# Ten input loads issued as 121 rows and 7 rows instead of 128 rows at once

## Chip, cores and metric

The kernel runs on one core of one Trainium2 chip. Its time is the device time of that core in microseconds (us); lower is better. Five engines work side by side on one program, each in its own order: PE (matmul, with its weight loads PEld), DVE, ACT, POOL, and SP, which in this kernel only issues DMAs. The core has 16 DMA engines that move the data.

## What is computed

For 8 batches, 12 heads, 448 positions and a head size of 64, all in float32 at the borders:

```python
scores = scale * np.matmul(q, k.transpose(0, 1, 3, 2)) - np.log(S)
attn = 1.0 / (1.0 + np.exp(-scores))
x = np.matmul(attn, v)            # heads side by side: x is [8, 448, 768]
wq = x @ w_q                      # [8, 448, 64]
wk = x @ w_k
W_tok = scale * np.einsum('bsd,btd->bst', wq, wk)
mixed = np.einsum('bst,btd->bsd', W_tok, x)
out = np.maximum(mixed, 0.0) @ w_out
```

## The kernel before

The 12 heads of a batch are taken four at a time, which gives 24 quads, n = 0 to 23. For each quad the kernel loads q, k and v (448 KB each, float32), casts them to bfloat16 (mostly on POOL), brings q and k into transposed form (transposes on PE or DVE), and makes seven blocks of scores: PE multiplies (line 328), one ACT instruction per block takes the sigmoid of 128 x 896 numbers out of PSUM (line 333), and PE multiplies the result with v (line 350). When three quads of a batch are done, the token-mixing part of that batch follows, and its output is stored.

The order of the work on every engine is written out by hand. The string `PLAN` gives one letter per step, `ORDER` gives the order of the loads and of their casts, and `BANKS` names the PSUM banks. "k5" below is the k load of quad 5.

Loads go through `load1`, which `pump_loads` calls on SP. A load is one DMA of 128 rows, 3.5 KB to a row: line 177 for q and k of the quads that are transposed on DVE (each row one piece of 896 numbers), line 188 for v and the other q and k (each row two pieces of 448 numbers). All loads share a pool of 8 buffers (`p_ld`), so a load is issued only when the load eight places before it has been cast:

```python
            if len(ring) >= 8 and ring[-8] not in cast:
                break
```

SP works in order: a DMA that has to wait holds up all DMAs behind it, including the loads, the copies of the output weights (`wout<-wout`, line 878) and the stores of the output.

The framework adds one more rule, which the source doesn't show. Each DMA that SP or ACT issues signals its landing on one of eight semaphores, called DMAHW0 to DMAHW7 in the lists below, and these are handed out in rotation, one per DMA. A DMA waits until the DMA that had its semaphore before it has landed. So no more than eight of these DMAs are under way at a time.

The cast of a load waits for all DMAs that fill its buffer. POOL casts at line 201 (q and k of the quads transposed on DVE), line 224 (other q and k) and line 218 (v). The weights `w_out` come in by two DMAs that POOL issues (line 670), on a queue of their own.

Of the kernel before, what the change touches and what calls it, by code (L numbers as in the profile page):

```python
# [17 lines left out]
def kernel(  # L18
# [17 lines left out]
    P = 128  # L36
    NI, NP = 7, 64
# [112 lines left out]
    SRC = dict(q=q, k=k, v=v)  # L150
# [3 lines left out]
    def arrange(n, eng):  # L154
# [12 lines left out]
        for g in range(2):  # L167
            lo = slice(64 * g, 64 * g + 32)
            eng.tensor_copy(out=w[lo, 1], in_=z[lo])  # L169

    def load1(n, nm, eng):
        u, j = quads[n]
        if KIND[n] in "cer" and nm != "v":
            t = p_ld.tile([P, 2 * RUN + PAD], F32, tag="ld", name=nm + "32")
            t = t[:, 0 : 2 * RUN] if n < SPLIT else t.rearrange("p (y x) -> p y x", y=2)[:, :, 0:RUN]
            rows = SRC[nm][u, 4 * j : 4 * j + 4]
            eng.dma_start(
                out=t,
                in_=rows.rearrange("h (p r) d -> (h p) (r d)", r=2 * NI)
                if n < SPLIT else rows.rearrange("h (p y r) d -> (h p) y (r d)", y=2, r=NI),  # L180
            )
            ld[nm, n] = (
                t.rearrange("p (y i e d) -> p e y i d", y=2, i=NI, e=2)
                if n < SPLIT else t.rearrange("p y (i e d) -> p e y i d", i=NI, e=2)
            )
            return
        t = p_ld.tile([P, 2, NI * HD], F32, tag="ld", name=nm + "32")
        eng.dma_start(
            out=t,
            in_=SRC[nm][u, 4 * j : 4 * j + 4].rearrange(  # L190
                "(g h) (p i) d -> (h p) g (i d)", g=2, i=NI
            ),
        )
        ld[nm, n] = t

# [486 lines left out]
    def cols(r):  # L682
# [9 lines left out]
        out=ident, in_=ident, compare_op=ALU.not_equal, fill=1.0, base=0,  # L692
# [35 lines left out]
    def pump_loads():  # L728
        while len(loaded) < len(ORDER):

            late = len(ring) > LATE
            if late and not allowed[0]:
                break
            nm, n = ORDER[len(loaded)]
            if nm == "w" and n or (nm, n) in CASTING:
                loaded.add((nm, n))
                continue
            if len(ring) >= 8 and ring[-8] not in cast:
                break
            allowed[0] -= late  # L740
            ring.append((nm, n))
            if nm == "w":
                load_weights()
            else:
                load1(n, nm, nc.sync)
            loaded.add((nm, n))
# [81 lines left out]
    for t in PLAN:  # L828
# [17 lines left out]
        elif kind == "P":  # L846
            n, i = divmod(c, NI)
# [17 lines left out]
        elif t == "z":  # L865
            n = quads_r.pop(0)
# [16 lines left out]
        elif kind == "M":  # L883
            u, x = divmod(c, NC // 2)
# [48 lines left out]
```

## Time and profile before

| | |
|---|---|
| median of 3 runs | 182.57 us (180.17 to 185.29) |
| profiled execution, span from first to last instruction | 180.1 us |
| busy in the span | PE 169.6, ACT 159.0, DVE 145.6, POOL 121.4 us |
| moved by DMA | 47.31 MB, mean 263 GB/s |
| granted TensorE clock | full throughout |

The profile gives no time of the profiled execution beside its span; the span lies at the lowest of the three timed runs. The profile's time line lists instructions in order of time as: start, duration, engine, line, what is written and read, count, and in brackets the idle time just before it and what ended that idle time. The view of stretches gives busy times of each engine between two points in time. The DMA view gives, for each group of issues, the count, the size and the median time from issue to landing.

### The profile page before, as it was taken

The page shows a single profiled execution, that of the slowest core. Times are in us where ns is not written, and L with a number is a line of the kernel's source. Part 1 is how long each engine was busy: PE and PEld are TensorE (multiplying, and loading weights), DVE is VectorE, ACT ScalarE, POOL GpSimd, SP SyncE. Part 2 cuts the span into 40 slices and gives each one's busy share as a digit, 9 for nine tenths or more (in the row PEclk, how much of TensorE's full clock was granted, in tenths as well). Part 3 has the DMA queues.
Part 4 walks back from the last instruction along what each step waited for, and adds up shares of the span by engine and source line. Part 5 has one row for each costly group of instructions (what it writes and reads, how often), then busy time and mean ns, then how long its engine had stood idle before and what let it go on. Part 6 is the DMA issues. An engine that isn't in the chain of part 4 may idle for free.

```text
span 180.1 us, 7907 instructions
## 1 busy us (share of the span) xinstructions
PE 169.6 (94%) x3440; PEld 112.2 (62%) x3440; DVE 145.6 (81%) x227; ACT 159.0 (88%) x208; POOL 121.4 (67%) x166
## 2 busy tenths in 40 slices
PE   7698899889899999999999999999999999999990
PEld 3334445444575555445667786678887788888660
DVE  3578899997989896889999999979898886768351
ACT  4699999999899999999999999999999989976300
POOL 1028799689999999999999999979979910010000
PEclk9999999999999999999999999999999999999999
DMA  5999999999999998899998889987795523505876
GB/s 177 355 372 349 322 383 381 280 302 356 342 294 349 339 265 267 217 319 365 343 300 315 217 288 305 342 322 213 200 338 173 135 64 73 137 4 122 201 208 175
DMA packets 27475, 47.31 MB, mean 263 GB/s; under 512 B 3888, under 2 KB 23600, under 8 KB 27440
## 3 DMA queue, kind: packets, MB, share of 16 engines
q1 hardware_dynamic: 26160, 44.64, 78.0%
q0 software_dynamic: 800, 1.18, 3.6%
q10 hardware_dynamic: 480, 0.98, 1.5%
q8 instruction: 27, 0.44, 1.0%
q14 instruction: 8, 0.07, 0.1%
HBM read 35.78 MB, written 11.01 MB: 260 GB/s over the span
## 4 chain that ended last, share of the span: by engine, by line
PE 56%; POOL 16%; DMA 15%; DVE 5%; ACT 2%; issue 2%; SPq 1%; POOLq 0%
PE banks L539 15%; PE banks L350 10%; PE banks L328 10%; PE banks L620 8%; DMA q<-in_q_dram 6%; POOL qk L201 5%; DMA w<-in_moe_w_k_dram 4%; DMA k<-in_k_dram 3%; POOL qk L169 3%; DMA wout<-wout 2%; ACT at L333 2%; POOL v L218 2%; PE banks L579 2%; PE banks L413 2%; POOL swap L163 2%
## 5 line engine op out<-in xcount | busy, mean ns | idle before, releaser
L333 ACT ACTIVATE at<-banks 128x896 bf16<-128x896 f32 x168 | 140.0, 948 | 3.4 <-PE banks L328 3.0
L328 PE MATMUL banks<-qk 64*64 64x448 bf16 x672 | 62.2, 358 | 3.3 <-ACT at L333 1.6
L350 PE MATMUL banks<-at,v 64*64 64x448 bf16 x672 | 47.3, 351 | 0.8 <-ACT at L333 0.7
L328 PEld LDWEIGHTS <-qk 64*64 64x64 bf16 x672 | 25.9, 105 | 20.7 <-issue 13.2
L539 PE MATMUL banks<-wout,mx 64*64 64x384 bf16 x672 | 36.6, 323 | 0.0
L201 POOL CAST qk<-k 128x896 bf16<-128x896 f32 x19 | 22.8, 1199 | 10.6 <-DVE qk L302 9.7
L350 PEld LDWEIGHTS <-v 64*64 64x64 bf16 x672 | 23.2, 107 | 8.6 <-issue 1.7
L539 PEld LDWEIGHTS <-mx 64*64 64x64 bf16 x672 | 23.3, 107 | 4.5 <-issue 0.5
L359 DVE CAST xt<-banks 128x896 bf16<-128x896 f32 x22 | 23.8, 1083 | 2.3 <-PE banks L350 1.8
L620 PE MATMUL banks<-wout,mx 128*128 128x384 bf16 (+1 forms) x138 | 24.4, 320 | 0.0
L480 DVE TENSOR_SCALAR mx<-banks 128x1024 bf16<-128x1024 f32 (+3 forms) x22 | 21.3, 972 | 1.9 <-PE banks L493 0.7
L201 POOL CAST qk<-q 128x896 bf16<-128x896 f32 x17 | 20.4, 1198 | 2.6 <-DMA q<-in_q_dram 1.3
L218 POOL CAST v<-v 128x896 bf16<-128x896 f32 x22 | 20.6, 950 | 1.4 <-DMA v<-in_v_dram 0.4
L620 PEld LDWEIGHTS <-mx 128*128 128x128 bf16 x138 | 12.3, 98 | 9.8 <-issue 3.2
L285 DVE STREAM_TRANSPOSE qk<-qk 128x448 f32<-128x448 f32 x28 | 17.0, 627 | 0.4 <-POOL qk L166 0.3
L163 POOL COPY swap<-qk 32x448 uint32<-32x448 uint32 x28 | 15.5, 554 | 2.3 <-DVE qk L201 0.7
L166 POOL COPY qk<-qk 32x448 uint32<-32x448 uint32 x28 | 15.8, 566 | 1.6
L169 POOL COPY qk<-swap 32x448 uint32<-32x448 uint32 x28 | 15.8, 564 | 1.6
L254 DVE STREAM_TRANSPOSE qk<-qk 32x448 f32<-32x448 f32 x24 | 15.3, 636 | 0.6
L422 POOL COPY wq<-wqk 64x448 bf16<-64x448 bf16 x3 | 1.7, 555 | 15.7 <-DVE wqk L421 15.7
L653 DVE COPY o<-banks 128x384 f32<-128x384 f32 x12 | 6.6, 553 | 5.7 <-PE banks L620 5.3
L653 ACT COPY o<-banks 128x384 f32<-128x384 f32 x9 | 4.4, 490 | 7.1 <-PE banks L620 6.9
(91 smaller groups left out, 206.5 us busy)
## 6 DMA issues: line engine op xcount, KB each, us to landing
q<-in_q_dram SPq DMA_DIRECT2D x24, 448.0 KB, 6.6
v<-in_v_dram SPq DMA_DIRECT2D x24, 448.0 KB, 6.3
k<-in_k_dram SPq DMA_DIRECT2D x23, 448.0 KB, 7.0
out_dram<-o SPq DMA_DIRECT2D x50, 192.0 KB, 3.9
wout<-in_moe_w_out_dram POOLq DMA_DIRECT2D x2, 576.0 KB, 12.2
wout<-wout SPq DMA_DIRECT2D x12, 96.0 KB, 6.2
out_dram<-o ACTq DMA_DIRECT2D x4, 192.0 KB, 3.5
k<-in_k_dram SPq DMA_DIRECT2D x1, 256.0 KB, 5.6
```

The costliest lines, as they stand in the source:

```text
L163: eng.tensor_copy(out=z[lo], in_=w[hi, 0])
L169: eng.tensor_copy(out=w[lo, 1], in_=z[lo])
L201: COPY[e](out=f[:, :, "qk".index(nm)].rearrange("p e i d y -> p e y i d"), in_=ld.pop((nm, n)),)
L218: COPY[e](out=t16.rearrange("p b i d -> p (b i d)"), in_=ld.pop((nm, n)).rearrange("p b x -> p (b x)"),)
L285: nc.vector.transpose(out=qk[n][:, t].rearrange("p t i n -> p (t i n)").bitcast(F32), in_=w)
L328: nc.tensor.matmul(sc[HALF[h], g, 0:S], qk[n][HALF[g], h, 1, i, :], qk[n][HALF[g], h, 0].rearrange("p i n -> p (i n)"), start=True, stop=True,
L333: inst = nc.scalar.activation(at, sc[:, :, 0:S], ACTF.Sigmoid, bias=attn_bias, scale=attn_scale)
L350: nc.tensor.matmul(ps[HALF[g], h, 0:S], ld["v16", n][HALF[h], g, i, :], ats[n, i][HALF[h], g, :], start=(i == 0), stop=(i == NI - 1),)
L359: read(fb, COPY[eng](out=xt(u, j)[:, :, 0:S], in_=ps[:, :, 0:S]))
L480: inst = nc.vector.tensor_scalar(dst, ps, moe_scale, 0.0, ALU.mult, ALU.max)
L539: nc.tensor.matmul(ps[HALF[x], y, 0:NB], mx[HALF[y], u, b, 64 * (i - 3 * y) : 64 * (i - 3 * y) + 64], wout16[HALF[y], slot(y, b), x * NB : ...
L620: nc.tensor.matmul(ps, mxs[w][:, 2 * S * c + m * P : 2 * S * c + (m + 1) * P], wout16[:, c, w0:w1], start=(c == 0), stop=(c == NC - 1),)
```

## The change

A load named in `THIN` is issued as two DMAs, rows 0 to 120 and rows 121 to 127, into the same buffer. All other loads stay as they are. The ten are k3, k5, q6, v5, v6, k8, v8, v9, k12 and v10.

```diff
+    THIN = "k3 k5 q6 v5 v6 k8 v8 v9 k12 v10".split()
+    CUT = 121
+
+    def load_rows(nm, n, eng, dst, rows):
+
+        if f"{nm}{n}" not in THIN:
+            eng.dma_start(out=dst, in_=rows)
+            return
+        for r in (slice(0, CUT), slice(CUT, P)):
+            eng.dma_start(out=dst[r], in_=rows[r])
...
-            eng.dma_start(
-                out=t,
-                in_=rows.rearrange("h (p r) d -> (h p) (r d)", r=2 * NI)
+            load_rows(
+                nm, n, eng, t,
+                rows.rearrange("h (p r) d -> (h p) (r d)", r=2 * NI)
...
-        eng.dma_start(
-            out=t,
-            in_=SRC[nm][u, 4 * j : 4 * j + 4].rearrange(
-                "(g h) (p i) d -> (h p) g (i d)", g=2, i=NI
-            ),
-        )
+        load_rows(
+            nm, n, eng, t, SRC[nm][u, 4 * j : 4 * j + 4].rearrange("(g h) (p i) d -> (h p) g (i d)", g=2, i=NI),
+        )
```

The order of instructions on PE, DVE, ACT and POOL stays the same. SP has ten more DMAs, and from the first split load on the eight semaphores fall to other DMAs. On SP, around quad 5 to 9, the rows before are these (v5, q7, v6, q8, k8, k9, q9; the brackets name what each waits for, its own landing semaphore among it):

```order
L188 DMA v_444<-in_v_dram 128x2x448 [waits DMAHW7_49,Pool_49]
L177 DMA q_478<-in_q_dram 128x896 [waits DMAHW0_49,Pool_49]
L188 DMA v_481<-in_v_dram 128x2x448 [waits DMAHW1_49,Pool_49]
L177 DMA q_486<-in_q_dram 128x896 [waits DMAHW2_49,Pool_49]
L177 DMA k_504<-in_k_dram 128x896 [waits DMAHW3_49,Pool_49]
L177 DMA k_662<-in_k_dram 128x896 [waits DMAHW4_49,Pool_49]
L177 DMA q_666<-in_q_dram 128x896 [waits DMAHW5_49,Pool_49]
```

The same loads on SP after the change, v5, v6 and k8 in two parts each:

```order
L180 DMA v_447<-in_v_dram 121x2x448 [waits DMAHW2_49,Pool_49]
L180 DMA v_447<-in_v_dram 7x2x448 [waits DMAHW3_49]
L177 DMA q_482<-in_q_dram 128x896 [waits DMAHW4_49,Pool_49]
L180 DMA v_485<-in_v_dram 121x2x448 [waits DMAHW5_49,Pool_49]
L180 DMA v_485<-in_v_dram 7x2x448 [waits DMAHW6_49]
L177 DMA q_491<-in_q_dram 128x896 [waits DMAHW7_49,Pool_49]
L180 DMA k_509<-in_k_dram 121x896 [waits DMAHW0_49,Pool_49]
L180 DMA k_509<-in_k_dram 7x896 [waits DMAHW1_49]
L177 DMA k_668<-in_k_dram 128x896 [waits DMAHW2_49,Pool_49]
L177 DMA q_672<-in_q_dram 128x896 [waits DMAHW3_49,Pool_49]
```

The load k9 (k_662 before, k_668 after) had DMAHW4 and waited for the DMA eight places before it, the load q6. It now has DMAHW2, which the 121 rows of v5 had before it, so it waits for the landing of a load that stands only five loads ahead of it.

## The prediction

> **What bounds the kernel now.** I read the busy shares first, then the time line of the engine that is nearest to full, then the engines that feed it. The first lines of the page:
>
> ```profile
> span 180.1 us, 7907 instructions
> PE 169.6 (94%) x3440; PEld 112.2 (62%) x3440; DVE 145.6 (81%) x227; ACT 159.0 (88%) x208; POOL 121.4 (67%) x166
> DMA  5999999999999998899998889987795523505876
> ```
>
> PE and ACT are both nearly full over the whole span, so the next question is who is full when. The DMA row (40 slices of 4.5 us, tenths of the 16 engines) says that the DMA engines are full from 5 us to about 70 us, which is the part where the ten loads lie. The time line of ACT for this part:
>
> ```profile
> 9.17 39.00 ACT L333 ACTIVATE at<-banks 128x896 bf16<-128x896 f32 x48 [0.21 <-PE banks L328]
> 48.65 13.22 ACT L333 ACTIVATE at<-banks 128x896 bf16<-128x896 f32 x16 [0.48 <-PE banks L328]
> 62.22 1.73 ACT L333 ACTIVATE at<-banks 128x896 bf16<-128x896 f32 x2 [0.34 <-PE banks L328]
> ```
>
> ACT takes 48 sigmoids in 39.00 us without a gap, from 9.17 to 48.17, and then idles 0.48 us. Stretches of the span tell who takes over (the columns are the stretch, its length, the busy us of PE, PEld, DVE, ACT and POOL, clock, DMA share, GB/s):
>
> ```profile
> core 0: us, PE busy (x) PEld busy (x) DVE busy (x) ACT busy (x) POOL busy (x), PEclk, DMA share, GB/s
> 25.00:30.00 5.00, 4.85 (x74) 2.75 (x75) 4.76 (x9) 5.00 (x7) 5.00 (x6) 1.00 1.05 384
> ...
> 50.00:170.00 120.00, 119.86 (x2607) 85.33 (x2598) 102.47 (x150) 112.70 (x150) 87.76 (x121) 1.00 0.78 241
> ```
>
> From 50 to 170 us PE is busy 119.86 of 120.00 us. So **ACT sets the pace to 48 us and PE from 50 us on**. Both are full, and what comes earlier than it comes now buys almost nothing: of ACT's idle time before PE takes over there are 0.21 + 0.48 = 0.69 us, with the 0.34 at 62 us 1.03 us. That is the ceiling of any gain by faster loads in this execution.
>
> What comes later is another matter. POOL casts the loads, and its time line shows who waits for whom:
>
> ```profile
> 15.74 0.93 POOL L224 CAST k<-k 128x896 bf16<-128x896 f32 x1 [0.35 <-DMA k<-in_k_dram]
> ...
> 17.90 1.21 POOL L201 CAST qk<-k 128x896 bf16<-128x896 f32 x1 [0.18 <-DMA k<-in_k_dram]
> ...
> 20.64 0.93 POOL L218 CAST v<-v 128x896 bf16<-128x896 f32 x1 [0.40 <-DMA v<-in_v_dram]
> 22.33 2.17 POOL L769 CAST wqk<-w 64x384 bf16<-64x384 f32 x4 [0.76 <-DMA w<-in_moe_w_k_dram]
> ...
> 36.33 1.20 POOL L201 CAST qk<-q 128x896 bf16<-128x896 f32 x1 [1.29 <-DMA q<-in_q_dram]
> ...
> 44.76 1.21 POOL L201 CAST qk<-k 128x896 bf16<-128x896 f32 x1 [0.30 <-DMA k<-in_k_dram]
> ```
>
> Six times between 15 and 45 us POOL stands idle until a load lands, 3.28 us in all, and the last of these (k9, at 44.76) is the last of the first half. Until then the casts run at the pace of the DMA engines; after it no cast up to 80 us waits for a load. The short way from that last wait to ACT: DVE waits for the cast of k9 and q9, and PE and ACT come right after.
>
> ```profile
> 44.49 1.17 DVE L278 STREAM_TRANSPOSE qk<-qk 128x448 f32<-128x448 f32 x2 [1.07 <-POOL qk L201]
> ```
>
> DVE idles 1.07 us here, within 4 us of ACT's 0.48. So the time has little slack against **later** landings near 45 us: what k9 and q9 lose there, ACT loses too, and PE behind it.
>
> **The change part by part: the issue.** Ten more DMAs on SP. One issue costs about what these rows of SP show (start, duration):
>
> ```profile
> 5.64 0.38 SPq L188 DMA_DIRECT2D k<-in_k_dram  x1
> 12.18 0.37 SPq L188 DMA_DIRECT2D v<-in_v_dram  x1
> ...
> 24.53 0.37 SPq L188 DMA_DIRECT2D v<-in_v_dram  x1
> 25.80 0.34 SPq L177 DMA_DIRECT2D q<-in_q_dram  x1
> ...
> 29.52 1.20 SPq L177 DMA_DIRECT2D k<-in_k_dram  x2
> ```
>
> That is 10 x 0.38 = 3.8 us of SP, in ten places. SP waits for casts and landings most of the time (6.2 us between the two rows at 5.64 and 12.18), and a load takes far longer to land than that, because a queue of loads stands before it. I take 0. If the queue were empty, each issue would cost its 0.38 us.
>
> **The bytes per DMA engine.** A load of 448 KB is 128 rows; spread over 16 engines that is 8 rows, 28 KB, on each. At 384 GB/s (the stretch 25 to 30) one engine moves 24 GB/s, so a load costs each engine 448 x 1024 / 384 = 1.19 us and one row costs 0.15 us. How 121 and 7 rows are spread no row of the trace shows: every load in it has 128 rows. The ends: if the rows are dealt out one by one, no engine has more than 9 rows, and a split load costs at most 0.15 us more. If only equal shares are made, 121 = 11 x 11 gives 11 engines 11 rows each and the 7 rows go one each to seven engines. If these are seven of the eleven, seven engines carry 12 rows instead of 8 (+4 x 0.15 = **+0.60 us** per split load), four carry 11 (+0.45), and five carry none (-1.19). I take the second, the dearer end, since no row excludes it. [...]
>
> Six of the ten (k3, k5, q6, v5, v6, k8) go ahead of k9. The extra of k3 falls into SP's pause before 12.18, in which the engines work off the queue, so five count: 5 x 0.60 = **3.0 us** more on seven engines by the time that k9 lands. The other four (v8, v9, k12, v10) come when no cast waits for a load: 0.
>
> Against that stands work that is not a load. The page's third part:
>
> ```profile
> q1 hardware_dynamic: 26160, 44.64, 78.0%
> ...
> q8 instruction: 27, 0.44, 1.0%
> ```
>
> The 27 fetches of instructions are 16 KB each and took 1.0% of 16 x 180.1 us, so 28.8 / 27 = 1.07 us of one engine each, one every 6.7 us: seven by 45 us, about as much as a load's share each. A load has landed when its last engine is done. If the engine that has the fetches is always the same, it is up to 7 us behind the others less what it makes good in pauses, and it is this engine that ends the waits of POOL. If it is one of the five that are spared, five split loads take 5 x 1.19 = 6.0 us off it. That all loads then come earlier by 1 to 2 us until 42 us, and k9 with the +3.0 of the seven others about when it does now, is my estimate. The gain in time is small either way: between 0 and the 0.48 us of ACT at 48.65. I take half, **-0.25 us**.
>
> **The eight semaphores.** The two halves of a load use up two of them, so SP looks less far ahead. k9 now waits for v5. The DMA view for v5 (issued 24.53) and k9 (the second of the pair at 29.52, so 30.4) and the smallest load in the empty queue at the start:
>
> ```profile
> v<-in_v_dram SPq DMA_DIRECT2D x1, 448.0 KB, 9.5
> ...
> k<-in_k_dram SPq DMA_DIRECT2D x1, 448.0 KB, 14.2
> ...
> k<-in_k_dram SPq DMA_DIRECT2D x1, 192.0 KB, 3.4
> ```
>
> v5 lands at 34.0, so k9 is issued 3.6 us later than at 30.4. In this trace it landed at 44.6, behind q7, v6, q8 and k8: 4 x 1.19 = 4.8 us of queued work on the engines that carry all of it, more than the 3.4 us in which a load lands from an empty queue. I take 0; the price, if the cover were gone, is at most the 3.6 us. Behind k9 on SP wait q9, v7 and q10, then the copies of the weights, which PE doesn't read in this part.
>
> **Sum.** 0 (issue) - 0.25 (landings) + 0 (semaphores) on the profiled span of 180.1. The median of the runs is 2.47 us above that span; I put the difference onto the median: 182.57 - 0.25 = 182.3.
>
> **The rivals.**
> - *The slow side: the extra rows pace the casts.* If the engine with the fetches is one of the eleven, nothing is relieved. It carries the fetches and the extra rows, k9 and q9 land 3.0 us later, DVE, PE and ACT have no slack there: +3.0, so 185.6. With the semaphores' cover gone instead, +3.6: 186.2; with both, +6.6: 189.2. It decides from the point where k9 lands later than 44.7, when POOL already waits for it. For it speaks that five of sixteen engines are fewer than eleven; against it that an engine behind the others has less to do in each pause of SP.
> - *The relief reaches further.* The median run is 2.4 us above the fastest. If in such a run ACT waits for late loads, the relief would give part of that back: up to 182.57 - 2.4 = 180.2. Nothing in this trace shows such a run.
> - *No uneven spread.* Rows dealt out evenly: 5 x 0.15 = 0.75 us at most on some engines, nothing on the path but that: 182.6 to 183.3.
>
> **How the numbers follow.** The forecast, within 1.0 us of the median, has 0.50; even spread 0.13; the slow rival 0.25, half of it past 186.2; the far relief 0.12. Two per cent (3.65 us) is about what a measurement of this kernel can tell from no change, since its runs spread by 2.8%. That gives slower 0.14 (half of the slow rival, and a little for the spread of the runs), faster 0.07 (part of the far relief, with the spread in its favour), same 0.79. The range goes from the far relief, 180.0 with the span itself as its floor, to the slow rival with one of its prices, 186.2; beyond lie some 0.12 above and 0.05 below.
>
> **What would show it.** Right: SP with 10 more DMAs; POOL's wait before the cast of q7 (1.29 us) shorter, its wait for k9 about the same; ACT's gap near 48 us between 0 and 0.7; PE full from 50 to 170. The slow rival would show as POOL waits for loads of over 1 us at 40 to 47 and an ACT gap of 2 us or more near 48. Even spread would show as landings unchanged to 0.2 us. I am wrong if the time moves by more than 3.65 us, above all if PE is no longer full after 50 us.

## The result and the profile after

The change takes **196.63 us** (median; 193.0 to 199.75), the kernel before in the same measurement 182.63 us (180.17 to 185.29). The ratio is **1.0705, with a 95% interval of 1.0638 to 1.0773**: 7% or 12.9 us slower, and far outside the predicted 180.0 to 186.2. The ratio leaves out runs that were disturbed, and the profiled execution of the change (197.57 us) is one of them, while the undisturbed runs took 193.0 to 195.69 us.

The first part of its page (span, busy time of the engines, DMA row in 40 slices), and from the fifth part the sigmoid:

```profile
span 195.8 us, 7921 instructions
PE 174.5 (89%) x3439; PEld 117.2 (60%) x3440; DVE 145.2 (74%) x227; ACT 160.6 (82%) x208; POOL 122.2 (62%) x166
...
DMA  6999999999997689999999988997879533603875
...
L341 ACT ACTIVATE at<-banks 128x896 bf16<-128x896 f32 x168 | 141.7, 934 | 17.3 <-PE banks L336 16.7
```

(The lines are eight higher here: L333 is now L341, L328 is L336, L201 is L209, L218 is L226, L224 is L232.) The same group of before:

```profile
L333 ACT ACTIVATE at<-banks 128x896 bf16<-128x896 f32 x168 | 140.0, 948 | 3.4 <-PE banks L328 3.0
```

The engines do the same work, but ACT stands idle ahead of its sigmoids for 17.3 us instead of 3.4. These 13.9 us are most of the 15.7 us by which the span grew. Where they lie, ACT's time line of the change says (the bracket is the idle time and its releaser):

```profile
9.05 1.73 ACT L341 ACTIVATE at<-banks 128x896 bf16<-128x896 f32 x2 [0.23 <-PE banks L336]
...
20.54 14.12 ACT L341 ACTIVATE at<-banks 128x896 bf16<-128x896 f32 x17 [1.29 <-PE banks L336]
...
42.65 8.45 ACT L341 ACTIVATE at<-banks 128x896 bf16<-128x896 f32 x10 [4.10 <-PE banks L336]
52.25 4.30 ACT L341 ACTIVATE at<-banks 128x896 bf16<-128x896 f32 x5 [1.15 <-PE banks L336]
...
58.43 0.92 ACT L341 ACTIVATE at<-banks 128x896 bf16<-128x896 f32 x1 [1.88 <-PE banks L336]
```

Where before one run of 48 sigmoids went from 9.17 to 48.17 without a gap, there are now pieces. POOL, which casts the loads, shows what they wait for:

```profile
18.70 0.94 POOL L232 CAST k<-k 128x896 bf16<-128x896 f32 x1 [1.62 <-DMA k<-in_k_dram]
...
36.35 0.94 POOL L232 CAST q<-q 128x896 bf16<-128x896 f32 x1 [2.01 <-DMA v<-in_v_dram]
...
46.26 1.20 POOL L209 CAST qk<-q 128x896 bf16<-128x896 f32 x1 [1.22 <-DMA q<-in_q_dram]
...
54.44 2.31 POOL L209 CAST qk<-k 128x896 bf16<-128x896 f32 x2 [1.08 <-DMA k<-in_k_dram]
```

All four wait for landings, for 1.1 to 2.0 us (the second is the cast of q6, where the profile names the landing of a v load). The first is k3, cast at 15.74 before: 3.0 us later. The pair at 54.44 is k8, one of the ten, and k9. Before, k9 was cast at 44.76, and k8 at 43.25 without a wait:

```profile
43.25 1.20 POOL L201 CAST qk<-k 128x896 bf16<-128x896 f32 x1
```

Both come some **11 us later**, and now it is the landing of k8 that POOL waits for. The transposes on DVE at 55.67 (44.49 before) start when the cast of k8 ends, and wait 2.86 us for POOL instead of 1.07:

```profile
55.67 1.17 DVE L286 STREAM_TRANSPOSE qk<-qk 128x448 f32<-128x448 f32 x2 [2.86 <-POOL qk L209]
```

In stretches of the span (length, busy us of PE, PEld, DVE, ACT, POOL, clock, DMA share, GB/s), of the change:

```profile
25.00:45.00 20.00, 15.55 (x258) 8.32 (x253) 14.89 (x21) 15.21 (x19) 12.28 (x15) 0.85 1.02 260
40.00:45.00 5.00, 4.46 (x94) 2.95 (x94) 3.04 (x3) 2.21 (x3) 2.58 (x3) 0.50 1.04 242
62.00:182.00 120.00, 118.05 (x2594) 86.63 (x2587) 99.51 (x147) 111.63 (x148) 87.88 (x120) 0.98 0.78 236
```

and the first of them in the kernel before:

```profile
25.00:45.00 20.00, 18.54 (x358) 9.69 (x358) 18.27 (x26) 20.00 (x26) 17.59 (x22) 1.00 1.08 335
```

This pair of rows holds the answer's outline. The DMA engines are as busy as before (1.02 against 1.08), but move 260 GB/s instead of 335: a byte costs 335/260 x 1.02/1.08 = 1.22 times as much of their time. The change adds no bytes. After PE has waited, the granted clock is lower as well: 0.50 from 40 to 45 us, though PE is busy again for 4.46 of these 5.00 us. From 62 us on PE is full again (118.05 of 120.00 us), and the loss is not made good.

### The profile page after: what moved, and what is told of

Read it like the earlier page. It is cut to its first block, busy times and chain, and to the rows that moved or that the text cites. A ratio compares the mean times of both kernels' runs of the same rounds, so it can differ in the third digit from the quotient of the medians.

```text
span 195.8 us, 7921 instructions
## 1 busy us (share of the span) xinstructions
PE 174.5 (89%) x3439; PEld 117.2 (60%) x3440; DVE 145.2 (74%) x227; ACT 160.6 (82%) x208; POOL 122.2 (62%) x166
## 4 chain that ended last, share of the span: by engine, by line
PE 56%; DMA 32%; POOL 6%; SPq 2%; issue 1%; DVE 1%; POOLq 0%; DVEq 0%
PE banks L547 14%; DMA k<-in_k_dram 14%; DMA q<-in_q_dram 11%; PE banks L336 10%; PE banks L358 10%; PE banks L628 9%; DMA v<-in_v_dram 8%; PE banks L587 2%; PE banks L421 2%; PE banks L380 2%; PE banks L396 1%; PE banks L477 1%; PE banks L433 1%; PE banks L501 1%; POOL qk L209 1%
## 5 line engine op out<-in xcount | busy, mean ns | idle before, releaser
L341 ACT ACTIVATE at<-banks 128x896 bf16<-128x896 f32 x168 | 141.7, 934 | 17.3 <-PE banks L336 16.7
L336 PE MATMUL banks<-qk 64*64 64x448 bf16 x672 | 65.9, 374 | 5.1 <-DVE xn L409 2.4
L358 PE MATMUL banks<-at,v 64*64 64x448 bf16 x672 | 49.6, 363 | 2.3 <-POOL v L226 1.8
L336 PEld LDWEIGHTS <-qk 64*64 64x64 bf16 x672 | 27.3, 108 | 22.5 <-issue 14.6
L358 PEld LDWEIGHTS <-v 64*64 64x64 bf16 x672 | 25.4, 110 | 9.0 <-POOL v L226 2.9
L209 POOL CAST qk<-k 128x896 bf16<-128x896 f32 x19 | 22.7, 1200 | 12.6 <-DMA k<-in_k_dram 11.2
L628 PE MATMUL banks<-wout,mx 128*128 128x384 bf16 (+1 forms) x138 | 25.3, 328 | 1.3 <-DVE xn L409 1.3
L226 POOL CAST v<-v 128x896 bf16<-128x896 f32 x22 | 21.2, 979 | 5.4 <-DMA v<-in_v_dram 2.6
L209 POOL CAST qk<-q 128x896 bf16<-128x896 f32 x17 | 20.4, 1200 | 5.1 <-DMA q<-in_q_dram 2.0
```

The lines of the kernel that those rows point to most:

```text
L209: COPY[e](out=f[:, :, "qk".index(nm)].rearrange("p e i d y -> p e y i d"), in_=ld.pop((nm, n)),)
L226: COPY[e](out=t16.rearrange("p b i d -> p (b i d)"), in_=ld.pop((nm, n)).rearrange("p b x -> p (b x)"),)
L336: nc.tensor.matmul(sc[HALF[h], g, 0:S], qk[n][HALF[g], h, 1, i, :], qk[n][HALF[g], h, 0].rearrange("p i n -> p (i n)"), start=True, stop=True,
L341: inst = nc.scalar.activation(at, sc[:, :, 0:S], ACTF.Sigmoid, bias=attn_bias, scale=attn_scale)
L358: nc.tensor.matmul(ps[HALF[g], h, 0:S], ld["v16", n][HALF[h], g, i, :], ats[n, i][HALF[h], g, :], start=(i == 0), stop=(i == NI - 1),)
L628: nc.tensor.matmul(ps, mxs[w][:, 2 * S * c + m * P : 2 * S * c + (m + 1) * P], wout16[:, c, w0:w1], start=(c == 0), stop=(c == NC - 1),)
```

## The experiments

Two explanations stood at the start. Either the loads themselves take longer (by unequal shares of the engines, or because a packet is slower when the rows are not all 128), or the ten extra DMAs do harm as such, by their issue and by the landing semaphores that they use up. Unless an edit says otherwise, all else is as in the change.

**Equal shares: 112 and 16 rows.**

```diff
-    CUT = 121
+    CUT = 112
```

> The same ten loads are cut into 112 and 16 rows, so SP issues the same ten extra DMAs and the eight semaphores rotate in the same way, but both parts have a number of rows that 16 divides. Theory A (the parts of 121 and 7 rows go to 11 and 7 of the 16 DMA engines, and that unequal share makes the loads late): within 2 us of before, about 183, and packets up by 160 (10 x 16 more semaphore writes) instead of 20. Rival B (the extra DMAs and the semaphores make SP look less far ahead): as slow as the change, 193 to 198.

190.0 us against 181.49, ratio 1.0507 (1.0411 to 1.0602). Neither number came: most of the loss stays though the shares are equal. That they are equal, the count of packets says, if each engine that a DMA uses adds one small packet of its own: the kernels of loads alone (below) have 128 packets under 512 B for eight loads of 128 rows and 88 for eight loads of 121 rows, 16 and 11 to a load. Page of before, of the change, and of this kernel:

```profile
DMA packets 27475, 47.31 MB, mean 263 GB/s; under 512 B 3888, under 2 KB 23600, under 8 KB 27440
```

```profile
DMA packets 27495, 47.31 MB, mean 242 GB/s; under 512 B 3908, under 2 KB 23620, under 8 KB 27460
```

```profile
DMA packets 27635, 47.31 MB, mean 254 GB/s; under 512 B 4048, under 2 KB 23760, under 8 KB 27600
```

The change has 20 more than before, ten times 11 + 7 - 16; 112 and 16 rows have 160 more, ten times 16 + 16 - 16. The 11 and 7 engines of the prediction fit these rows, and the trace of the change has the same numbers: up to 18.6 us, just before k3 is cast at 18.70, its two parts signal their landing 11 and 7 times, where a load of 128 rows before does so 16 times (k9 from 39.7 to 44.6 us). The stretch 25 to 45 us of this kernel:

```profile
25.00:45.00 20.00, 16.89 (x326) 8.88 (x319) 15.98 (x23) 19.26 (x24) 14.72 (x19) 1.00 1.09 273
```

The engines are just as busy and move 273 GB/s instead of 335: they are slower per byte, with all sixteen in use by that count.

**120 and 8 rows.**

```diff
-    CUT = 121
+    CUT = 120
```

> The same ten loads are cut into 120 and 8 rows: if the number of engines is the largest divisor up to 16, 15 engines carry 8 rows and 8 of them one row more, so no engine has more than 9 rows. Theory A, by the count of rows alone: +0.15 us per load, 183 to 184.5. Rival C (any DMA on fewer than 16 engines brings the engines out of step and slows the packets of all of them): 190 or more, with 3.5 KB packets that take much longer than their 140 ns. Rival B: 193 to 198.

191.79 us, ratio 1.0582 (1.0487 to 1.0678); 70 more packets than before, ten times 15 + 8 - 16.

**88 and 40 rows.**

```diff
-    CUT = 121
+    CUT = 88
```

> The same ten loads are cut into 88 and 40 rows: 11 engines with 8 rows, then 10 engines with 4 rows, so ten engines carry 12 rows and five none, as unequal as 121 and 7 and a little more, but in blocks of 8 and 4 rows. Theory A: as slow as the change or slower, 196 to 202. Rival D (the blocks of 11 rows fall across the groups of rows that an engine otherwise writes, and that is what slows the packets): clearly faster than the change, 184 to 190.

199.56 us, ratio 1.0973 (1.0870 to 1.1075); 50 more packets, ten times 11 + 10 - 16. The less equal the shares, the worse, it seems. If the parts use the same engines as far as they can, the fullest engine has 8 rows of a load with 112 + 16 (5.1%), 9 with 120 + 8 (5.8%), 12 with 121 + 7 (7.1%) and 12 with 88 + 40 (9.7%). But each of these four cuts pays, even that with equal shares. The unequal shares of the change are worth about the difference of 7.05 and 5.07%, 2.0% or 3.6 us, with intervals of about 0.7 and 1.0% on the two, if the packets are slowed alike in both.

**Only k3 is cut.**

```diff
-    THIN = "k3 k5 q6 v5 v6 k8 v8 v9 k12 v10".split()
+    THIN = "k3".split()
```

> Only k3, the first of the ten, is cut into 121 and 7 rows. In the trace of the change the cast of k3 already began 3.0 us later than before. Theory A with the extra rows alone (+0.6 us on seven engines): within 1 us of before. If one cut load by itself makes what follows late by about 3 us, which nothing later makes up for: 184 to 187.

183.87 us against 181.49, ratio 1.0144 (1.0063 to 1.0225): 2.6 us from one load, with an interval of 1.1 to 4.1. POOL's cast of k3 and ACT behind it, in this kernel:

```profile
17.73 0.93 POOL L232 CAST k<-k 128x896 bf16<-128x896 f32 x1 [2.18 <-DMA k<-in_k_dram]
```

```profile
19.57 1.73 ACT L341 ACTIVATE at<-banks 128x896 bf16<-128x896 f32 x2 [1.53 <-PE banks L336]
21.82 2.54 ACT L341 ACTIVATE at<-banks 128x896 bf16<-128x896 f32 x3 [0.53 <-PE banks L336]
24.78 39.13 ACT L341 ACTIVATE at<-banks 128x896 bf16<-128x896 f32 x48 [0.43 <-PE banks L336]
```

k3 is cast 2.0 us later than before (17.73 against 15.74), and ACT, which had no gap at all here, idles 1.53 + 0.53 + 0.43 = 2.49 us. Over the whole span a part is made good: ACT's idle time ahead of the sigmoids is 5.0 us against 3.4, 1.6 more, and the span is 1.7 us longer.

Why one load costs that much, the stretch from 12 to 17 us tells, first of before, then of this kernel:

```profile
12.00:17.00 5.00, 4.31 (x80) 2.02 (x80) 4.39 (x7) 5.00 (x7) 3.16 (x5) 1.00 0.98 341
12.00:17.00 5.00, 3.99 (x75) 1.72 (x74) 3.72 (x7) 5.00 (x8) 1.87 (x2) 1.00 1.05 241
```

For 5 us the full engines move 241 GB/s instead of 341. That is 1.20 MB, and k3 has only 0.46 MB of it. k3 comes in pieces of 1.75 KB. The packets of 3.5 KB in this stretch belong to loads that are not cut, and in the trace their median is 234 ns here (64 packets), against 140 ns before (192 packets); in the change it is 225 ns (37 packets). **So the cut load slows whole loads beside it.**

**Only the late four are cut.**

```diff
-    THIN = "k3 k5 q6 v5 v6 k8 v8 v9 k12 v10".split()
+    THIN = "v8 v9 k12 v10".split()
```

> Only the last four of the ten (v8, v9, k12, v10) are cut into 121 and 7 rows. The prediction put them at 0, because no cast waits for a load after 45 us: 181 to 183. If their slower packets hold up the loads beside them beyond the margins of 3 to 5 us: 184 to 188.

186.42 us against 181.68, ratio 1.0248 (1.0188 to 1.0308): 4.5 us (3.4 to 5.6), not 0. DVE of this kernel, then of before, then ACT of this kernel:

```profile
68.03 0.66 DVE L209 CAST qk<-q 128x896 bf16<-128x896 f32 x1 [3.68 <-DMA q<-in_q_dram]
```

```profile
65.26 0.88 DVE L201 CAST qk<-q 128x896 bf16<-128x896 f32 x1
```

```profile
70.78 0.92 ACT L341 ACTIVATE at<-banks 128x896 bf16<-128x896 f32 x1 [3.02 <-PE banks L336]
```

A cast of q on DVE that waited for nothing now waits 3.68 us for its load (q12, which comes behind the four in the order of the loads), and ACT idles 3.02 us behind it. Over the whole span ACT's idle time ahead of the sigmoids is 8.0 us against 3.4, 4.6 more: about the loss.

**The same ten loads cut by columns:** two DMAs of 128 rows, each with half of every row.

```diff
-        for r in (slice(0, CUT), slice(CUT, P)):
-            eng.dma_start(out=dst[r], in_=rows[r])
+        for y in range(2):
+            if len(dst.shape) == 3:
+                eng.dma_start(out=dst[:, y], in_=rows[:, y])
+            else:
+                c = slice(y * RUN, (y + 1) * RUN)
+                eng.dma_start(out=dst[:, c], in_=rows[:, c])
```

> The same ten loads are cut by columns: two DMAs of all 128 rows, half a row each (1792 bytes). The ten extra DMAs on SP and the rotation of the semaphores are those of the change, only the rows per DMA are 128 again. Rival B (extra DMAs, semaphores, SP looks less far ahead): 188 to 192, as with 112 and 16 rows. [...]

182.12 us against 181.68, ratio **1.0004** (0.9963 to 1.0044). Its stretch and its ACT:

```profile
25.00:45.00 20.00, 18.59 (x369) 9.67 (x366) 18.41 (x27) 20.00 (x26) 17.86 (x22) 1.00 1.08 335
```

```profile
6.44 41.60 ACT L345 ACTIVATE at<-banks 128x896 bf16<-128x896 f32 x51 [0.95 <-PE banks L340]
```

335 GB/s as before, and 51 sigmoids without a gap, to 48.04. Ten more DMAs, with the same use of the semaphores, cost nothing: this rival falls.

**Rows 0 to 63 and rows 64 to 127.**

```diff
-        for r in (slice(0, CUT), slice(CUT, P)):
+        for r in (slice(0, 64), slice(64, P)):
```

> The same ten loads are cut into 64 and 64 rows, 4 rows per engine in each part, perfectly even. Rival B: 188 to 192, as with 112 and 16. [...] Only equal shares mattering: 181 to 184.

193.34 us, ratio 1.0579 (1.0479 to 1.0680), 264 GB/s from 25 to 45 us at a DMA share of 1.09. So equal halves are slow too, with the engines as full as before (1.08 at 335 GB/s).

**The even rows and the odd rows.** This tells apart the number of rows and which rows they are.

```diff
-        for r in (slice(0, CUT), slice(CUT, P)):
+        for r in (slice(0, P, 2), slice(1, P, 2)):
```

> The ten loads are cut into the 64 even and the 64 odd rows of the buffer, two DMAs each, equal shares on all 16 engines. [...] If any DMA of 64 rows is slow: 191 to 196, as with the two halves.

182.01 us against 181.64, ratio **1.0011** (0.9969 to 1.0053), with this stretch:

```profile
25.00:45.00 20.00, 18.59 (x366) 9.55 (x363) 19.01 (x28) 20.00 (x26) 17.34 (x22) 1.00 1.08 337
```

Two DMAs of 64 rows cost nothing as long as each reaches over the whole tile. **For parts of 64 rows it is which rows that decides, not how many, nor how many DMAs there are.** The rows that are read alternate here too; the second of the kernels below changes the rows written alone.

**Loads alone, by their number of rows.** Three kernels hold nothing but loads of the same kind, eight to a stage, one stage after the other. The first has this loop (the rows of its stages in PHASES):

```python
    for phase in PHASES:
        for x in range(8):
            ...
            for a, b in ([(0, 121), (121, 128)] if x in (1, 4) else [(0, 128)]) if phase == "mix" else phase:
                nc.sync.dma_start(out=bufs[x][a:b], in_=rows[a:b])
        for x in range(7, -1, -1):
            nc.vector.tensor_copy(out=sink[:, x : x + 1], in_=bufs[x][:, 0:1])
```

> No computation at all, only loads of 3.5 KB rows from HBM, eight to a stage and a wait between stages: 128 rows, 112, 121, 120, 64, 112 and 16 in two DMAs, 128 again, 88, 96, and 128 with two of the eight cut into 121 and 7. The output is zeros. [...] Theory A alone (shares): 112, 96 and 64 rows at 140 ns, and only 121, 120 and 88 slower in GB/s, in proportion to the engines they use.

Its stages after the first one, each from the first issue to the last landing (columns: length, DVE, POOL, clock, DMA share, GB/s), for loads of 112, 121, 120 and 64 rows, 112 + 16, 128, 88 and 96 (the last stage, "mix", overlaps the stores of the output and is left out):

```profile
15.80:29.20 13.40, 0.05 (x1) 0.00 (x0) 1.00 0.91 240
30.40:50.40 20.00, 0.01 (x1) 0.00 (x0) 1.00 0.65 173
51.30:67.20 15.90, 0.00 (x0) 0.00 (x0) 1.00 0.82 216
68.40:79.10 10.70, 0.02 (x1) 0.00 (x0) 1.00 0.80 172
80.30:96.00 15.70, 0.11 (x2) 0.00 (x0) 1.00 0.84 234
96.80:108.90 12.10, 0.05 (x1) 0.00 (x0) 1.00 0.82 303
110.10:125.30 15.20, 0.00 (x0) 0.00 (x0) 1.00 0.62 167
126.50:138.20 11.70, 0.04 (x1) 0.00 (x0) 1.00 0.87 235
```

112 rows take longer than 128 (13.40 us against 12.10; the 128 rows of the next two kernels, behind their first stage, take 12.48 to 12.89). The time of one row's packet is share x 16 engines x length / rows: for 128 rows 0.82 x 16 x 12.10 / (8 x 128) = 155 ns, for 112 rows 0.91 x 16 x 13.40 / 896 = 218 ns, for 121 rows 0.65 x 16 x 20.00 / 968 = 215 ns, for 64 rows 0.80 x 16 x 10.70 / 512 = 267 ns. The lower share with 121 rows (0.65) fits eleven busy engines of sixteen (0.69); the longer packet comes on top.

**Loads alone, by which rows.** The same loop with other stages, R being a slice:

```diff
+        [R(0, 128)], [R(0, 64)], [R(64, 128)], [R(0, 128, 2)], [R(0, 128)], [R(0, 64), R(64, 128)], [R(0, 128, 2), R(1, 128, 2)],
```

> Loads alone again, eight to a stage: 128 rows; 64 rows from HBM into rows 0 to 63 of the buffer; into rows 64 to 127; into every second row; 128 rows again; both halves as two DMAs; even and odd rows as two DMAs. The output is zeros. What is read from HBM is 64 rows in one piece in the second to fourth stage, only the rows that are written differ. If the slow packets come from the HBM side or from the mere number of 64 rows: the same 270 to 280 ns in all three. [...]

The source of a stage with 64 rows is 64 rows in one piece each time, so only the rows written differ. The stages after the first one: rows 0 to 63; rows 64 to 127; every second row; all 128; both halves; even and odd rows:

```profile
15.30:26.38 11.08, 0.00 (x0) 0.00 (x0) 1.00 0.78 166
27.30:38.35 11.05, 0.00 (x1) 0.00 (x0) 1.00 0.77 166
39.25:47.92 8.67, 0.00 (x0) 0.00 (x0) 1.00 0.67 212
48.80:61.69 12.89, 0.00 (x1) 0.00 (x0) 1.00 0.78 285
63.00:80.45 17.45, 0.00 (x0) 0.00 (x0) 1.00 0.89 210
81.30:95.67 14.37, 0.00 (x1) 0.00 (x0) 1.00 0.87 302
```

A half takes 0.78 x 16 x 11.08 / 512 = 270 ns for a packet, whichever half it is; 64 rows spread over the tile take 0.67 x 16 x 8.67 / 512 = 182 ns, near the 157 ns of all 128 in this kernel. Whole loads as two halves move 210 GB/s, in one piece 285. So with 64 rows it is the rows written that make the packets slow, not what is read. The last stage (even and odd rows) overlaps the first stores of the output, 302 GB/s x 14.37 us being 0.67 MB more than its loads have; so its 14.37 us are an upper bound, still 3.1 us below the halves' 17.45.

Against the 157 ns of all 128 rows, a packet of a half takes 1.7 times as long (270 / 157) and one of every second row 1.2 times (182 / 157); with 112 or 121 rows it was 1.4 times (218 and 215 against 155). Why the rows written matter no run shows.

**Do the cut loads slow their neighbours too?** One load cost 2.6 us in the kernel, 0.6 in the prediction. The same loop with mixed stages:

```diff
+        [FULL] * 8, [FULL, THIN, FULL, FULL] * 2, [FULL] * 8, [FULL, HALVES, FULL, FULL] * 2,
+        [THIN] * 8, [[R(0, 32)]] * 8, [[R(0, 128, 4)]] * 8, [FULL] * 8,
```

> Loads alone, eight to a stage with a wait between stages, the output zeros: all 128 rows; the same with two of the eight cut into 121 and 7 rows; 128 again; two of the eight cut into halves of 64; all eight cut into 121 and 7; 32 rows into rows 0 to 31; 32 rows into every fourth row; 128 again. If only the cut loads themselves are slow, the second stage takes about 2 us longer than the first (each cut load 1 us, from 18.6 us for eight loads of 121 rows against 10.6 us for eight of 128). If they slow the whole loads beside them as well: 3 us or more. Every fourth row should run like 128 rows by packet, 32 rows in one block much slower.

The stretches of the stages from the second on, each as long as DVE waited for its loads: two loads of eight cut as 121 + 7; all whole; two of eight cut in halves; all eight cut as 121 + 7; 32 rows (0 to 31); 32 rows (every fourth); all whole:

```profile
14.11:28.80 14.69, 0.01 (x1) 0.00 (x0) 1.00 0.83 250
29.65:42.45 12.80, 0.01 (x1) 0.00 (x0) 1.00 0.79 287
43.32:59.19 15.87, 0.01 (x1) 0.00 (x0) 1.00 0.77 231
60.05:82.12 22.07, 0.01 (x1) 0.00 (x0) 1.00 0.63 166
83.32:89.57 6.25, 0.01 (x1) 0.00 (x0) 1.00 0.58 148
90.45:97.36 6.91, 0.01 (x1) 0.00 (x0) 1.00 0.48 133
98.23:110.71 12.48, 0.00 (x1) 0.00 (x0) 1.00 0.82 295
```

Two cut loads add 14.69 - 12.80 = 1.9 us (2.2 against the last stage), about 1 us each; eight add 22.07 - 12.64 (the mean of the whole stages) = 9.4, or **1.2 us each, twice the predicted 0.60**. So by the length of its stage a load cut as 121 + 7 costs about the same among whole loads as among its like. The packets say that the neighbours are slowed all the same, as in the kernel with k3: a packet takes 158 ns with all loads whole (0.79 x 16 x 12.80 / 1024) and 217 ns with all cut. If neither kind touched the other, six whole loads and two cut ones would give (6 x 158 + 2 x 217) / 8 = 173 ns. Measured are 0.83 x 16 x 14.69 / 1024 = 191 ns.

Halves behave otherwise: 1.5 to 1.7 us each for two of eight, but (17.45 - 12.89) / 8 = 0.57 us each when all eight are halves. That stays open. The two stages of 32 rows (6.91 us spread over the tile, 6.25 in one block) tell nothing of packets by their length, since the engines are busy for only 0.48 and 0.58 of them; by the same working a packet takes 207 ns when the rows are spread and 227 ns in the block (medians in the trace: 140 and 194 ns).

## Why the prediction was wrong

- **The step that failed is the landings, -0.25 us in the sum, and in it the price of a cut load, +0.60 us.** The sum let all five times 0.60 count for nothing, on the ground that an engine with the fetches ends each load later anyhow. No run shows such cover: k3 is cast 3.0 us later than before, k8 11 us. The price itself was rows on the fullest engine times 0.15 us a row, with the 0.15 us taken from whole loads and held fixed. The number of engines, an assumption there, was right (11 and 7, by the packet counts and the landing signals of k3; which ones, they don't tell). The price of a row was not: a DMA of 112 or 121 rows takes 215 to 218 ns for a packet against 155, so a cut load costs 1.0 to 1.2 us among loads alone, and it slows whole loads beside it (234 ns against 140 for 3.5 KB with k3 alone cut). Equal shares with slow packets (112 + 16) already cost 5.07%. The unequal shares cost about 3.6 us more for all ten loads, near the 3.0 us that the prediction had for five; that part was about right. The upper bound of the range had no term for slower packets, though each load in the trace had 128 rows and could say nothing of others.
- **"The extra of k3 falls into SP's pause": wrong.** k3 alone costs 2.6 us. SP's pause is no pause of the DMA engines, whose share before was 0.97 to 1.11 in every microsecond from 9 to 13. POOL had waited 0.35 us for k3 before, so there was no cover, and its 2.0 us went on to ACT. They are more than the 1.0 to 1.2 us of a cut load among loads alone; the whole loads that ran slow beside it are a part of them, how large was not separated.
- **The way from k9 to ACT was read off another load's row.** The wait of 1.07 us on DVE at 44.49 ends with the cast of k8 (43.25 to 44.45), before the cast of k9 begins at 44.76. So DVE waits there for k8, which is itself one of the cut loads; the prediction took it for k9 and q9.
- **"The other four come when no cast waits for a load: 0": wrong.** They cost 4.5 us by themselves. The reading looked at POOL; the casts that run on DVE were left out, and the one at 65.26 comes 2.8 us later behind the four cut loads, with ACT idle behind it.
- **The slow rival had the path, not the size.** POOL waits of over 1 us for loads and an ACT gap near 48 were its signs, and they are there: 1.22 us on POOL at 46.26, 4.10 us on ACT at 42.65. Its price was 3.0 to 6.6 us; the loss is 12.9. Its reason, extra rows on some engines, was the smaller part (about 3.6 us).
- **The issue and the eight semaphores, 0 each: right.** With ten more DMAs on SP and the same use of the semaphores, the columns give 1.0004 and the even and odd rows 1.0011. Whether the semaphores cost something once the packets are slow was not separated.
- **The relief for the engine with the fetches, -0.25 us: not tested.** Nothing of it shows: POOL waits longer for loads, not shorter.
- **"PE full from 50 us on" held from 62 us only.** ACT waits for PE's scores at 52.25 and 58.43. The granted clock was lower too (0.50 from 40 to 45, a mean of 0.956 against 1.000 in the profiled executions); how much of the loss is the clock's share was not separated. k3 alone (2.6) and the late four (4.5) leave about 6 us for the other five, if the parts add up, which was not tried.
- **The sum set a span against a time.** In every run whose span is on record the time is 1.7 to 1.9 us above it. So an execution with a span of 180.1 took about 182 us (an estimate), near the median and not 2.47 us below it, and the span is no floor for the time. The forecast of 182.3 doesn't change by this.
- **What stays open is why** packets of DMAs of 96 to 121 rows take 1.4 times as long (212 to 218 ns against 155), with 112 rows at a DMA share of 0.91 as with 121 at 0.65. For halves the runs show that it is the rows written (270 ns against 182, with 64 rows read in one piece both times), though not why; for these the slowness is only measured.

## What to carry to other kernels

A load that is cut by rows can cost more than its bytes, because its packets can go slower (155 to 158 ns with all 128 rows, 215 to 218 with 112 or 121, 270 with 64 in one block, 182 with every second row), and with them those of the loads beside it (234 ns against 140): here, in a stage where the DMA engines are full, ten loads of 448 KB cut as 121 + 7 rows cost 7%, as 112 + 16 rows 5%, as two halves 6%. Cut by columns with all 128 rows in each part, or by even and odd rows, they cost nothing measurable here, so these are the cuts to try first. Before a late landing is priced at nothing, look at every engine that casts or reads loads, and ask of each number taken from a trace whether the changed instruction is still of the kind from which it was read. Check also which load a row belongs to before a chain of waits is built on it.

## What the hardware showed beyond that

- A load of 112 rows takes longer than one of 128 rows (eight: 13.40 us against 12.10 to 12.89), though it moves an eighth less.
- One load cut as 121 + 7 rows slows whole loads beside it: their packets of 3.5 KB had a median of 234 ns from 12 to 17 us with k3 cut, 140 ns before.
- Engines can be full and slow: a DMA share of 1.02 at 260 GB/s in the changed kernel, 1.08 at 335 before. The share alone does not tell how much is moved.
- The clock can fall after PE has stood still: in the change PE did nothing from 38 to 40 us, and the granted clock was 0.50 from 39 to 45. It doesn't fall at each wait: from 12 to 25 us PE was busy for 9.38 of 13.00 us at a clock of 1.00.
